# A new order for the passage from attention to the experts: logits, row copy, one-hot rows, and expert ranks in PSUM

## The chip, the core and the metric

One core of a Trainium2 chip runs the whole program in one launch. The metric is the device time of one execution in microseconds; the time before is the median of three runs. The five engines work side by side, each through its own queue in order: TensorE (PE, products into PSUM), VectorE (DVE), ScalarE (ACT), GpSimd (POOL) and SyncE (SP, which issues most transfers).

## What is computed

Causal attention with a bias from a running sum, then a routed layer of 16 experts over the 4608 tokens that attention leaves:

```python
scores = scale * q @ k.T + minimum(-(cum_i - cum_j), 0)     # causal
x = softmax(scores) @ v                                     # (8 * 576, 512)
g_idx = argmax(x @ w_group);  e_idx = argmax(x @ w_expert[g_idx])
combined = softmax weight of the group * softmax weight of the expert
out[token] = combined * (relu(x @ w1[g, e]) @ w2[g, e])     # one expert for each token
```

## The kernel before

**Attention** runs over 64 heads, two to a pair (32 pairs), in steps, one head a step. Each step emits its pieces by an order written out by hand as a string of letters (`ORDERS`, `FIRST`, `LAST`): a letter pops the next entry of a queue of that name. Of the letters that the change touches, for a pair p: W turns the reciprocal sums back, K divides (`finish`, xT, L362), O transposes the rows on TensorE (`rows_out`, L406) and o copies them out of PSUM (`leave`, xr, L412), X rounds xT to the high part (xTh, L375), L takes the low part (xTl, L379), M copies the tail (xtl, L384), and Q runs products of the router's logits. For the last batch of four pairs, three of the four chunks of logits are run early (L727, L728), on the Q of pair 30, the fourth in the router's `batch`. Steps 64 to 68 have no head left to score and only empty the queues. The O transpositions share one PSUM bank (`small`).

**Router** (class `Router`, `batch`): for each of 8 batches it transposes logits, finds the best group and expert (eq, oh), makes one-hot rows (hot, L822), counts them with TensorE (pc, L829), works out positions, and adds token numbers and weights to lists with products (pi, pw, L873) and an addition (`st.added`, L879). The exponents of the softmax need df (L887) on VectorE and an exponential on ScalarE (L889).

**Experts**: `moe` runs 16 slots. Each weight piece of 1 MB is loaded by SP (L995), rounded on ScalarE (wh, L997), and its low part is made on GpSimd (wl, L1000) or, from a rounded copy in PSUM (pw, L1005), on VectorE (L1007). The first expert is known before the last batch is routed: its rows of seven batches are gathered early, and a tile of remaining rows (`rest`) is gathered when the last batch's ids exist. Its items are: `h_items`, the hidden products (ph, L1107; first of four blocks, last of four blocks, twice), Relu (hh, L1102) and its rest (hl, L1103); `y_items`, the output products (py, L1168: a block of 16 products each for four columns, then the low weights); `rest.items()`, for the remaining rows: transposition (L1249), hidden products (L1263) and so on. The order of the remaining 15 experts is found on VectorE by ranks: a comparison of all keys with all keys (L1326), rank (L1327), a one-hot table sel (L1329), and its product with the expert numbers (L1332), summed to esl (L1333) and copied to integers (esi, L1335), from which SP reads where the next weights lie. The PSUM pool of transpositions (`pt[0]`, three banks) serves the weight copies pw, the gathered rows' transpositions and the rest's products.

**Order.** Up to step 62 all engines follow the hand-written order. Behind it, only TensorE does, in each part; the order of VectorE, ScalarE and GpSimd is set by a planner from its own estimate of times, in which an instruction emitted earlier goes first among those that are ready. Three helpers bend it: `behind(tc, later, earlier)` puts one instruction behind another in the order and adds no wait on another engine; `hold` adds a wait; `after` does the same as `behind` for a group.

Of the kernel before, what the change touches and what calls it, by code (L numbers as in the profile page):

```python
# [8 lines left out]
F32 = mybir.dt.float32  # L9
# [4 lines left out]
ALU = mybir.AluOpType  # L14
AX = mybir.AxisListType
# [4 lines left out]
B, H, S, D = 8, 8, 576, 64  # L20
P = 128
# [3 lines left out]
E = 16  # L25
# [88 lines left out]
def attention(tc, qk, v, s, wr, xs, st):  # L114
    nc = tc.nc
    NP = B * H // 2
    LEAD = 4
    with ExitStack() as ctx:
# [215 lines left out]
        def normalise(p, vals, sums):  # L334

            c = p % 4
            m = {}

            def turn():
                for k in "YZWK":  # L340
                    need(k, p - 1)
                m["f"] = sm.tile([P, S], F32, name=f"st{p}", tag="st", bufs=1)
                nc.vector.transpose(m["f"], sums)
                push("Z", p, recip)

            def recip():
                f = m["f"]
                rc = m["rc"] = sm.tile([P, S // 32], F32, name=f"rc{p}", tag="rc", bufs=2)
                nc.vector.reciprocal(rc, f.rearrange("p (b c) -> p b c", c=32)[:, :, 0])

                push("W", p, back)

            def back():
                nc.vector.transpose(m["f"], m["rc"].unsqueeze(2).to_broadcast([P, S // 32, 32]))
                push("K", p, finish)

            def finish():
                for k in "OXLM":
                    need(k, p - 2)
                x = m["x"] = sm.tile([P, S], F32, name=f"xT{p}", tag="xT", bufs=2)  # L360
                xTs[p] = x
                st.divided = nc.vector.tensor_tensor(out=x, in0=vals, in1=m["f"], op=ALU.mult)  # L362
                push("X", p, high)
                push("O", p, lambda: rows_out(p))

            def high():
                x = m["x"]
                if c == 0:
                    for k in "LMQ":
                        need(k, p - 1)  # L370
                    rt.read(p // 4)
                    xhl[p // 4] = [late.tile([P, 4, 512], F32R, name=f"xT{n}{p}", tag=f"xT{n}", bufs=1) for n in "hl"]
                    xtail[p // 4] = XT[p // 4 % 2]
                xh, xl = (t[:, c] for t in xhl[p // 4])
                st.xh = nc.scalar.copy(xh, x[:, 0:512])  # L375
                push("L", p, lambda: low(xh, xl, x))

            def low(xh, xl, x):
                (nc.gpsimd if p < NP - 2 else nc.vector).tensor_tensor(  # L379
                    out=xl, in0=x[:, 0:512], in1=xh.bitcast(F32), op=ALU.subtract)  # L380
                push("M", p, lambda: tail(x))

            def tail(x):
                nc.scalar.copy(xtail[p // 4][:, 64 * c:64 * c + 64], x[:, 512:576])  # L384
                b = p // 4
                if p == NP - 2:
                    push("Q", p, lambda: rt.logits(b, *xhl[b], range(3)))
                if c == 3:
                    push("Q", p, lambda: route(b))

            push("Y", p, turn)
# [130 lines left out]
        for t in VT:  # L522
# [19 lines left out]
        LAST = FIRST  # L542
        ORDER0 = "B0 b e A0 a T t B1 b D A1 a B2 b e A2 a B3 b e e A3 a B4 b e A4 a A5 a".split()
        for step in range(-LEAD, NH + 5):
            m, a = step + LEAD, step - 1
# [18 lines left out]
            if step >= 2 and step // 2 + 4 < NP:  # L564
                push("S", step // 2 + 4, lambda p=step // 2 + 4, part=step % 2: split(p, part, True))
            named = {"A": A, "B": Bq, "C": C}
            order = FIRST if step < 3 else ORDERS if step < NH - 1 else LAST
            for part in order[step % 2] if step > 0 else ORDER0:
                if part[0] in named:
                    for f in named[part[0]][int(part[1]):int(part[1]) + 1]:  # L570
# [66 lines left out]
class Router:  # L637
# [127 lines left out]
    def batch(self, b, xtail, xh, xl):  # L765
# [27 lines left out]
        for c in range(4):  # L793
# [25 lines left out]
                        op=ALU.is_equal)  # L819
        F4 = [P, NB, 4, 4]  # L820
        ohb = st.hot[:, b]
        V.tensor_tensor(out=ohb.rearrange("p t (g e) -> p t g e", e=4), in0=oh[:, :, 1:5],  # L822
                        in1=oh[:, :, 0].unsqueeze(3).to_broadcast(F4), op=ALU.mult)
        yield 2

        pc = (self.ps_s if b < B - 1 else self.ps_t)(f"pc{b}")
# [57 lines left out]
            st.routed = first_ids(nc, self.end, st, 0, 3, ((0, 2, 3, st.ids0[:, 2:3]), (1, 0, 3, st.ids1)))  # L884

        df = self.end.tile([P] + G[1:], F32, name=f"df{b}", tag="eq", bufs=1)
        V.tensor_tensor(out=df, in0=lgv, in1=mb, op=ALU.subtract)  # L887
        ex = df
        nc.scalar.activation(ex, df, AF.Exp)  # L889
        yield 1  # L890
# [33 lines left out]
def moe(tc, w1, w2, xs, st, out):  # L924
# [3 lines left out]
    with ExitStack() as ctx:  # L928
# [20 lines left out]
        def bc(t, ax, shape):  # L949
            return t.unsqueeze(ax).to_broadcast(shape)  # L950
# [337 lines left out]
        def run(items):  # L1288
            for f in items:
                f()  # L1290
# [31 lines left out]
        for k in range(2):  # L1322
            V.scalar_tensor_tensor(out=key, in0=st.first[:, k], scalar=(2 - k) * 1.0e6, in1=key, op0=ALU.mult,
                                   op1=ALU.add)
        rank = mc.tile([P, E], F32, name="rank")
        V.tensor_tensor(out=t3, in0=bc(key, 1, S3), in1=bc(key, 2, S3), op=ALU.is_gt)  # L1326
        V.tensor_reduce(out=rank, in_=t3, axis=AX.X, op=ALU.add)  # L1327
        sel = mq.tile(S3, BF16, name="sel")
        V.tensor_tensor(out=sel, in0=bc(rank, 1, S3), in1=bc(ie, 2, S3), op=ALU.is_equal)  # L1329
        esl = mc.tile([P, E], F32, name="esl")  # L1330
        csl = mc.tile([P, E], F32, name="csl")
        V.tensor_tensor(out=t3, in0=sel, in1=bc(ie, 1, S3), op=ALU.mult)  # L1332
        V.tensor_reduce(out=esl, in_=t3, axis=AX.X, op=ALU.add)  # L1333
        esi = mc.tile([P, E], I32, name="esi")
        nc.scalar.copy(esi, esl)  # L1335

# [29 lines left out]
        with tc.manual_schedule(engines={ENG.PE}):  # L1366
# [4 lines left out]
                behind(tc, i, st.left)  # L1371
            behind(tc, st.xh, wts[0].casts[2])
            behind(tc, wts[0].casts[3], st.xh)
            hold(tc, lows[0, 0, 0], st.divided)
            behind(tc, wts[0].casts[8], first.split[0])
            h = first.h_items()
            run(h[:12])
# [8 lines left out]
            behind(tc, st.added[0], first.rests[5])  # L1386
            behind(tc, st.weighing, first.rests[7])
            Y, R = first.y_items(), rest.items()
            run(Y[:2] + R[:1] + Y[2:4])

            behind(tc, st.listed[2], first.product)
            run(R[1:5] + Y[4:])
# [255 lines left out]
```

## Time and profile before

| what | us |
|---|---|
| three runs | 929.62, 918.28, 924.96 |
| median | 924.96 |
| profiled execution | 921.04 |
| its span, first to last instruction | 919.3 |
| TensorE busy | 855.2 (93%) |
| VectorE busy | 736.9 (80%) |
| ScalarE busy | 610.2 (66%) |
| GpSimd busy | 605.7 (66%) |

The mean granted clock of TensorE over the span is 0.986 of full speed. In a timeline a row is one instruction or a run of equal ones: start, duration, engine, line, operation, what is written from what, shapes, how many; in square brackets the idle time of the engine ahead of it and what ended that. A wait is put down to the event that came last. The attention ends near 440 us, the first expert's products begin near 451, and the loop over the other experts begins near 490.

### The profile page before, as it was taken

How to read it: one execution, taken by the hardware profiler on the slowest of the kernel's cores; microseconds unless marked ns; L12 is line 12 of the kernel's file. 1: busy time of each engine (PE TensorE's matmuls, PEld its weight loads, DVE VectorE, ACT ScalarE, POOL GpSimd, SP SyncE). 2: the span in 40 equal slices, each digit the busy share in tenths (PEclk: the TensorE clock that was granted, in tenths of full speed). 3: DMA queues.
4: the chain of work that ended last, by engine and by line, in shares of the span. 5: the costliest groups of instructions: out<-in, count | busy, mean ns of one | idle time of the engine just before them, and what ended most of it. 6: DMA issues, size and time to landing. Idle time of an engine off the chain costs nothing. (4 is left out here: it accounts for less than half of the span.)

```text
span 919.3 us, 17750 instructions
## 1 busy us (share of the span) xinstructions
PE 855.2 (93%) x5584; PEld 780.2 (85%) x5584; DVE 736.9 (80%) x1981; ACT 610.2 (66%) x1389; POOL 605.7 (66%) x748
## 2 busy tenths in 40 slices
PE   4899999999999999998798999999999999999995
PEld 2778788788888888886687999999999999999984
DVE  7666697787979798777578888899888899888871
ACT  5667777677777777775646566666767666767750
POOL 9666567666776758546665856766676776767650
PEclk9999999999999999999899999999999999999998
DMA  7899888888888888622544645545555545655510
GB/s 204 236 238 227 215 230 227 206 210 200 220 223 217 221 223 214 160 74 100 189 150 168 221 176 205 193 169 190 215 185 191 195 183 205 229 197 192 181 70 24
DMA packets 81877, 174.06 MB, mean 189 GB/s; under 512 B 9676, under 2 KB 45132, under 8 KB 73584
## 3 DMA queue, kind: packets, MB, share of 16 engines
q1 hardware_dynamic: 71664, 152.93, 57.8%
q0 software_dynamic: 7488, 18.89, 5.8%
q10 hardware_dynamic: 2624, 1.03, 0.5%
q8 instruction: 46, 0.75, 0.4%
q14 instruction: 55, 0.45, 0.2%
HBM read 108.97 MB, written 19.69 MB: 140 GB/s over the span
## 5 line engine op out<-in xcount | busy, mean ns | idle before, releaser
L1000 POOL TENSOR_TENSOR wl<-raw,wh 128x512 fp32r<-128x512 f32 x163 | 210.3, 1305 | 76.2 <-ACT wh L997 58.5
L227 DVE CUSTOM_DVE_ANT_0 mx<-pm,mask 128x192 bf16<-128x192 f32 (+4 forms) x320 | 127.3, 418 | 36.0 <-PE pm L219 33.3
L997 ACT CAST wh<-raw 128x512 fp32r<-128x512 f32 x256 | 155.3, 616 | 1.4 <-issue 1.4
L1107 PE MATMUL ph<-xl,wh 128*128 128x256 f32 (+13 forms) x512 | 145.3, 303 | 3.0 <-DVE xl L1079 3.0
L1107 PE MATMUL ph<-xh,wh 128*128 128x256 f32 (+13 forms) x512 | 144.8, 302 | 2.0 <-ACT xh L1078 1.7
L219 PE MATMUL pm<-WA 66*128 66x288 f32 (+4 forms) x384 | 124.8, 356 | 21.5 <-DVE mc L227 11.5
L275 PE MATMUL ps<-WA 68*128 68x320 f32 (+4 forms) x384 | 135.3, 356 | 4.8 <-DMA WA<-tl 4.6
L315 PE MATMUL po<-pt,VT 128*128 128x256 f32 (+3 forms) x512 | 120.9, 355 | 6.8 <-issue 4.2
L1168 PE MATMUL py<-hl,wh 128*128 128x256 f32 (+13 forms) x448 | 113.6, 302 | 1.7 <-DVE hl L1103 1.7
L1168 PE MATMUL py<-hh,wh 128*128 128x256 f32 (+13 forms) x448 | 112.9, 302 | 0.0
L277 PE MATMUL ps<-WB 128*128 128x320 f32 (+4 forms) x384 | 109.8, 299 | 0.0
L315 PE MATMUL po<-pu,VT 128*128 128x320 f32 (+1 forms) x384 | 107.5, 388 | 1.1 <-POOL pu L294 1.1
L1221 DVE STREAM_TRANSPOSE yr<-yT 32x384 f32<-32x384 f32 (+1 forms) x208 | 104.5, 502 | 4.2
L315 PEld LDWEIGHTS po<-pt,VT 128*128 128x128 f32 x512 | 88.4, 193 | 21.0 <-issue 5.0
L1074 DVE STREAM_TRANSPOSE xt<-xg 32x256 f32<-32x256 f32 (+1 forms) x208 | 102.5, 493 | 3.1
L1107 PEld LDWEIGHTS ph<-xl,wh 128*128 128x128 f32 x512 | 96.9, 189 | 5.9 <-DVE xl L1079 5.0
L1107 PEld LDWEIGHTS ph<-xh,wh 128*128 128x128 f32 x512 | 97.1, 190 | 3.8 <-ACT xh L1078 2.9
L219 PEld LDWEIGHTS pm<-WA 66*128 66x128 f32 (+1 forms) x384 | 69.1, 192 | 31.8 <-DVE mc L227 15.5
L294 POOL TENSOR_SCALAR_AFFINE_SELECT pt<-pt 128x128 f32<-128x128 f32 (+2 forms) x192 | 65.8, 354 | 43.7 <-ACT pt L285 40.5
L1102 ACT ACTIVATE hh<-ph 128x256 fp32r<-128x256 f32 (+13 forms) x128 | 53.6, 420 | 60.3 <-PE ph L1107 59.5
L161 POOL TENSOR_TENSOR WB<-r,hl 64x576 fp32r<-64x576 f32 x62 | 87.3, 1408 | 5.9 <-ACT hl L157 2.1
L1107 PE MATMUL ph<-xh,wl 128*128 128x256 f32 (+13 forms) x512 | 90.2, 299 | 0.0
(246 smaller groups left out, 2000.8 us busy)
## 6 DMA issues: line engine op xcount, KB each, us to landing
raw<-in_w_dram SPq DMA_DIRECT2D x64, 1024.0 KB
r<-in_qk_dram SPq DMA_DIRECT2D x32, 576.0 KB
WA<-hl SPq DMA_DIRECT2D x60, 288.0 KB
WB<-hl SPq DMA_DIRECT2D x60, 288.0 KB
VT<-in_v_dram SPq DMA_DIRECT2D x32, 384.0 KB
WB<-hl SPq DMA_DIRECT2D x64, 144.0 KB
xs<-xr SPq DMA_DIRECT2D x15, 512.0 KB
WA<-cumd SPq DMA_DIRECT2D x56, 4.5 KB
```

What stands on the lines that cost most here:

```text
L161: (nc.vector if p < 1 else nc.gpsimd).tensor_tensor(out=hl[:, 2] if part else WB[p % NBB][0:64, KA, h], in0=r[hr, part], in1=hl[hr, part]. ...
L219: nc.tensor.matmul(ps[:rows, :cw], WA[i][0:66, QA, h, QO + q0:QO + q0 + rows], WA[i][0:66, KA, h, QO + c0:QO + c0 + cw], start=True, stop= ...
L227: nc.vector.tensor_tensor_reduce(out=tmp[:rows, :cw], in0=ps[:rows, :cw], in1=mk[:rows], scale=1.0, scalar=-3.0e38 if c0 == 0 else mo, op0 ...
L275: nc.tensor.matmul(ps[:rows, o:o + w], WA[i][0:68, KA, h, QO + k0:QO + k0 + rows], WA[i][0:68, QA, h, QO + q0:QO + q0 + w], start=True, st ...
L277: nc.tensor.matmul(ps[:rows, o:o + w], WB[p % NBB][:, KA, h, k0:k0 + rows], WB[p % NBB][:, QA, h, q0:q0 + w], start=False, stop=True)
L315: nc.tensor.matmul(po[0][:, qa - base:qb - base], VT[p % NVT].rearrange("p t a d -> p (t a d)")[:, (3 * t + 1 + h) * 64:][:, 0:P], x[:, c: ...
L997: self.casts.append(nc.scalar.copy(h[:, j], raw[:, j]))
L1000: self.low = lows[self.u, i, j] = nc.gpsimd.tensor_tensor(out=l[:, j], in0=raw[:, j], in1=h[:, j].bitcast(F32), op=ALU.subtract)
L1074: V.transpose(dst[:, 0:n, :, j], src[:, 0:n, :, i])
L1107: self.product = nc.tensor.matmul(pss[f][:, :cap], w[f // 4][:, c, (f % 4) * P:(f % 4 + 1) * P], x[:, c, :cap], start=(c == 0 and w is sel ...
L1168: self.product = nc.tensor.matmul(pss[c][:, :cap], w[2 + f // 4][:, f % 4, c * P:(c + 1) * P], x[:, f, :cap], start=(f == 0 and w is self. ...
L1221: V.transpose(dst[:, 0:n, :, i], src[:, 0:n, :, j])
```

## The change

1. Behind step 65 the orders are replaced by `ENDS`: the even step runs W O o K X L M Q once, the odd one nothing. Q, which ran ahead of K, X, L, M, now stands behind them, so the three early chunks of logits are emitted in step 66, ahead of the last O (pair 31).
2. The tail copy of pair 31 on ScalarE is put behind the rounding xTh of pair 31. That one stood already behind the row copy of pair 30 and three weight casts.
3. The first subtraction of the first expert's weights on GpSimd is held until the low part xTl of pair 31, no longer until its division.
4. In the last batch, df goes behind the one-hot rows hot.
5. The ranks and a copy of the expert numbers lie in a PSUM bank of `pt[0]`; sel and its product with the numbers read them there. The addition of the weights to the lists (`st.added[2]`) goes behind esl.
6. The transposition of the rest's rows stands behind three of the first expert's output blocks, not two.

```diff
@@ finish, low, tail
-                st.divided = nc.vector.tensor_tensor(out=x, in0=vals, in1=m["f"], op=ALU.mult)
+                nc.vector.tensor_tensor(out=x, in0=vals, in1=m["f"], op=ALU.mult)
...
-                (nc.gpsimd if p < NP - 2 else nc.vector).tensor_tensor(
+                st.xl = (nc.gpsimd if p < NP - 2 else nc.vector).tensor_tensor(
                     out=xl, in0=x[:, 0:512], in1=xh.bitcast(F32), op=ALU.subtract)
...
-                nc.scalar.copy(xtail[p // 4][:, 64 * c:64 * c + 64], x[:, 512:576])
+                i = nc.scalar.copy(xtail[p // 4][:, 64 * c:64 * c + 64], x[:, 512:576])
+                if p == NP - 1:
+                    behind(tc, i, st.xh)
@@ attention
+        ENDS = ["W O o K X L M Q".split(), []]
...
-            order = FIRST if step < 3 else ORDERS if step < NH - 1 else LAST
+            order = FIRST if step < 3 else ORDERS if step < NH - 1 else LAST if step < NH + 2 else ENDS
@@ Router.batch
-        V.tensor_tensor(out=ohb.rearrange("p t (g e) -> p t g e", e=4), in0=oh[:, :, 1:5],
-                        in1=oh[:, :, 0].unsqueeze(3).to_broadcast(F4), op=ALU.mult)
+        hot = V.tensor_tensor(out=ohb.rearrange("p t (g e) -> p t g e", e=4), in0=oh[:, :, 1:5],
+                              in1=oh[:, :, 0].unsqueeze(3).to_broadcast(F4), op=ALU.mult)
...
-        V.tensor_tensor(out=df, in0=lgv, in1=mb, op=ALU.subtract)
+        i = V.tensor_tensor(out=df, in0=lgv, in1=mb, op=ALU.subtract)
+        if b == B - 1:
+            behind(tc, i, hot)
@@ moe
-        rank = mc.tile([P, E], F32, name="rank")
+        shared = pt[0].tile([P, 512], F32, name="rank", tag="pt")
+        rank, nums = shared[:, 0:E], shared[:, E:2 * E]
+        V.tensor_copy(nums, ie)
...
-        V.tensor_tensor(out=t3, in0=sel, in1=bc(ie, 1, S3), op=ALU.mult)
-        V.tensor_reduce(out=esl, in_=t3, axis=AX.X, op=ALU.add)
+        V.tensor_tensor(out=t3, in0=sel, in1=bc(nums, 1, S3), op=ALU.mult)
+        behind(tc, st.added[2], V.tensor_reduce(out=esl, in_=t3, axis=AX.X, op=ALU.add))
...
-            hold(tc, lows[0, 0, 0], st.divided)
+            hold(tc, lows[0, 0, 0], st.xl)
...
-            run(Y[:2] + R[:1] + Y[2:4])
+            run(Y[:3] + R[:1] + Y[3:4])
```

## Rows read from the trace of the kernel before

**Rows 1.** Waits of TensorE, 425 to 500 us: total, times, longest.

```profile
PE px L406 <- ACT xr L412: 3.7, 1, 3.7
PE px L1057 <- DVE wl L1007: 2.6, 1, 2.6
...
PE prr_x L1249 <- DMA xg<-xs,ids: 1.6, 1, 1.6
PE pc L829 <- DVE hot L822: 1.2, 1, 1.2
```

**Rows 2.** Waits of TensorE, 497 to 920 us, the longest total.

```profile
PE ph L1107 <- DVE xl L1079: 3.0, 8, 0.4
```

**Rows 3.** Timeline of TensorE: start, us, engine, line, operation [idle before].

```profile
444.31 1.12 PE L406 MATMUL px<-ident,xT 128*128 128x128 f32 x4 [3.65 <-ACT xr L412]
...
451.25 0.36 PE L1107 MATMUL ph<-xh,wh 128*128 128x256 f32 x1
```

**Rows 4.** Timeline of ScalarE, 443 to 457 us.

```profile
443.40 0.24 ACT L384 COPY xtl<-xT 128x64 f32<-128x64 f32 x1 [2.41 <-DVE xT L362]
443.67 0.58 ACT L412 COPY xr<-px 128x512 f32<-128x512 f32 x1
...
445.71 0.62 ACT L375 CAST xTh<-xT 128x512 fp32r<-128x512 f32 x1
446.23 2.70 ACT L997 CAST wh<-raw 128x512 fp32r<-128x512 f32 x5
...
456.87 0.29 ACT L889 ACTIVATE df<-df 128x100 f32<-128x100 f32 x1 [1.06 <-DVE df L887]
```

**Rows 5.** Timeline of VectorE, 433 to 458 us.

```profile
433.65 0.69 DVE L379 TENSOR_TENSOR xTl<-xT,xTh 128x512 fp32r<-128x512 f32 x1 [0.16 <-ACT xTh L375]
...
446.36 1.57 DVE L379 TENSOR_TENSOR xTl<-xT,xTh 128x512 fp32r<-128x512 f32 x1 [2.99 <-ACT xTh L375]
...
455.49 1.35 DVE L887 TENSOR_TENSOR df<-logit,lmx 128x100 f32<-128x100 f32 x1
456.75 1.30 DVE L822 TENSOR_TENSOR hot<-oh 128x80 bf16<-128x80 f32 x1
457.98 0.41 DVE L1103 SCALAR_TENSOR_TENSOR hl<-ph,hh 128x256 fp32r<-128x256 f32 x1
```

**Rows 6.** Timeline of GpSimd, 444 to 460 us.

```profile
444.86 5.46 POOL L1000 TENSOR_TENSOR wl<-raw,wh 128x512 fp32r<-128x512 f32 x4 [7.90 <-ACT wh L997]
450.26 1.38 POOL L1294 MEMSET xg<- 128x1536 f32 x1
451.60 7.60 POOL L1000 TENSOR_TENSOR wl<-raw,wh 128x512 fp32r<-128x512 f32 x6
```

**Rows 7.** Timeline of VectorE, the difference of the batch before.

```profile
419.54 0.26 DVE L887 TENSOR_TENSOR df<-logit,lmx 128x100 f32<-128x100 f32 x1
```

**Rows 8.** Timeline of VectorE, 478 to 488 us.

```profile
478.30 3.48 DVE L1329 TENSOR_TENSOR sel<-rank,ie 128x256 bf16<-128x256 f32 x1
481.81 4.15 DVE L1332 TENSOR_TENSOR t<-sel,ie 128x256 f32<-128x256 bf16 x1
...
486.33 1.28 DVE L1007 TENSOR_TENSOR wl<-raw,pw 128x512 fp32r<-128x512 f32 x2
```

**Rows 9.** Timeline of TensorE, first and last of 32 output products.

```profile
464.85 0.36 PE L1168 MATMUL py<-hh,wh 128*128 128x256 f32 x1
...
468.65 0.28 PE L1168 MATMUL py<-hl,wh 128*128 128x256 f32 x1
```

**Rows 10.** Line 1007, whole span: ns min/median/max, first and last start.

```profile
L1007 DVE TENSOR_TENSOR wl<-raw,pw x93: 674/687/690, 463.1 to 886.2; 128x512 fp32r<-128x512 f32 x93
```

**Rows 11.** Timeline of ScalarE, 486 to 489 us.

```profile
486.45 0.20 ACT L1335 CAST esi<-esl 128x16 int32<-128x16 f32 x1 [7.08 <-DVE esl L1333]
...
487.05 1.19 ACT L1189 COPY yT<-py 128x256 f32<-128x256 f32 x4
```

**Rows 12.** Stretch: us, busy PE, PEld, DVE, ACT, POOL, granted clock, DMA share, GB/s.

```profile
489.00:490.00 1.00, 1.00 (x7) 0.94 (x6) 0.74 (x3) 0.70 (x2) 0.00 (x0) 0.50 0.90 377
```

## The prediction

> **What bounds the kernel now.** I read the page first, then the waits of TensorE in two stretches, then the timelines of the five engines between them, last the granted clock microsecond by microsecond. Behind 497 us TensorE's longest entry of waits is 3.0 us over eight places [rows 2]: the expert stage is a full queue of products, and what is won ahead of it should arrive at the end undiminished. Between 425 and 500 us, in the passage from attention to the experts, four single waits stand: 3.7, 2.6, 1.6 and 1.2 us [rows 1], 9.1 together. The change aims at these four and at nothing else: the orders of steps before 66 stay, so neither attention up to there nor the expert loop has another instruction. The most that can be won is thus about 9 us of 921, plus what the clock gives back.
>
> **First wait: copy, logits, low part.** The transposition of pair 31 sits behind 3.65 us of idle [rows 3], so that of pair 30 ended at 444.31 - 3.65 = 440.66. Its bank is the only one, and the copy that empties it ran on ScalarE at 443.67, behind a tail copy of pair 31 that had itself waited 2.41 us for the divided rows [rows 4]. ScalarE was therefore free at 440.99 with a ready copy behind a blocked one. The change puts the tail copy behind the rounding xTh: the copy runs 440.99 to 441.57, three weight casts follow at 2.70/5 = 0.54 each [rows 4] until 443.2, and xTh starts when the divided rows come, 443.40, in place of 445.71: 2.3 us earlier, done at 444.02 with 0.62. VectorE's low part takes 0.69 with GpSimd idle and 1.57 beside it [rows 5]; the new hold keeps GpSimd away, so 0.69: it ends at 444.74 where it ended at 447.93. The last chunk of logits can start 3.2 us earlier.
>
> The six other logits products move from behind the last transposition into the hole in front of it. Their inputs of pair 30 are long there (the other low part was made at 433.65 [rows 5]). They issue no DMA. The hole from 440.66 to 443.40 is 2.74 us; before, they stood between the last transposition (444.31 + 1.12 = 445.43) and the low part's end, 447.93, so at most 2.5. They fit and cost nothing; were they late, the last transposition would be, one for one.
>
> What follows is ScalarE's queue: after xTh now the tail copy (0.24) and five casts (2.70), until 444.02 + 0.24 + 2.70 = 446.96; before it was 446.23 + 2.70 = 448.93 [rows 4]. The last row copy, its DMA to xs (ScalarE's own queue), the copy of the logits and the rest up to the first expert product at 451.25 [rows 3] hang behind these casts. I take 1.97 us. Bounds: nothing, if the casts cannot start before 444 for a reason that the trace hides; 3.2, if the planner now lets the row copy and the logits pass the five casts. I take the value between, as rows show that order of ScalarE.
>
> The hold itself puts ten subtractions on GpSimd behind the low part, and behind those the clearing of a gather buffer and the later gathers. Before they began at 444.86 [rows 6], now at 444.74: nothing lost. The fourth ends 5.46 later; its user is the product with wl, 32 products behind the first one (0.12 each, by [rows 9]), so 3.9 after 449.28, at 453.2: three us of cover. SP's next weight load waits for the same four and does not move either.
>
> **Second wait: one-hot rows ahead of exponents.** Before: difference 455.49 (1.35), then one-hot 456.75 (1.30), and TensorE's count waited 1.2 for it [rows 1, 5]. Both are slow because GpSimd subtracts beside them (451.60 to 459.2 [rows 6]); the batch before took 0.26 for the difference [rows 7]. Swapped and 1.97 earlier, one-hot runs 453.52 to 454.85, difference to 456.2. The count's stall goes almost wholly. But the exponent is queued on ScalarE ahead of the first Relu: it had waited 1.06 for the difference and started 456.87 [rows 4]. The difference moves only 1.97 - 1.30 = 0.65, so exponent 456.2, Relu from 456.5, the first rest hl about 456.8 to 457.2; it was at 457.98 [rows 5]. The second half of the hidden products needs that bank (`acc` has four banks for eight blocks). TensorE could be there at 449.28 + 48 x 0.12 + 0.5 for the count = 455.6, so a new wait of about 1.6 takes the place of the 1.2. Without it this half would have started at 458.73 less 1.97 less 1.23; with it at 457.2. So from here on the lead is **1.5**, not 3.2. Bounds: 3.2 if the Relu goes first; 0.6 if the later slots of VectorE stretch by another 0.9 between subtractions.
>
> One page speaks to this place. No row shows a two-input VectorE instruction that ran beside a GpSimd clearing alone; beside subtractions they cost 1.35 and 1.30. The Trainium skill, SBUF — State Buffer, Who interferes with whom, says that a VectorE instruction with two SBUF inputs is blocked by a GpSimd instruction that reads SBUF, not by one that only writes. By it, two instructions of the routing that would now fall beside the clearing at 450.26 would cost what they cost undisturbed, an estimate of 1 us more lead here. The sum does not count it.
>
> **Third wait: one more block of outputs ahead of the gathered rest.** TensorE waits 1.6 us for the gather [rows 1]. The ids that it needs move with the products and with VectorE's chain, both by about 1.5. Ahead of it now stand three blocks in place of two; 32 products take 468.65 - 464.85 + 0.12 = 3.92 [rows 9], so a block of 16 is 1.96, more than 1.63. The wait goes: **1.6**. Behind it the fourth block (1.96) still covers the rounding of the transposed rest (0.6 and 0.7 on ScalarE and VectorE, like xTh and xTl). Lower bound 0, if the ids do not move.
>
> **Fourth wait: ranks in PSUM, list of experts first.** sel took 3.48 and the product after it 4.15 for 256 columns [rows 8], beside subtractions on GpSimd; both stood behind the addition of weights at 478.03. An instruction with one operand in PSUM does not stretch so: hl from ph, also 256 columns, took 0.41 at 457.98 in the middle of subtractions [rows 5, 6], and wl from pw, twice the columns, lies between 674 and 690 ns in all 93 cases [rows 10]. So each should cost 0.45, and both now run in VectorE's idle stretch before the addition. What hung behind: wl at 486.33 [rows 8], whose bank the transposition of the next expert's rows waited 2.6 for [rows 1], and ScalarE, which sat 7.08 us at esi with Relu and output copies queued behind it, those at 487.05 [rows 11]. All of this falls to the pace of TensorE. The idle also cost clock: at 489 us the granted clock is 0.50, the lower of its two levels [rows 12]; about 3 us ran so. TensorE keeps one short wait, as the fourth transposition needs the first one's bank (output copies 1.2, rounding 0.5, low 0.5, against 1.5 of other work): I charge 0.5. So 2.6 - 0.5, plus 1.3 of the 1.5 that half clock over 3 us costs: **3.4**. Bounds 2.0 (the clock falls anyway) and 4.2. The copy of indices into the bank (16 columns) is off the path, and the bank it takes in the pool of three is free again before the second hidden block of the rest asks.
>
> **Sum.** 1.5 + 1.6 + 3.4 = 6.5 us. The profiled execution took 921.04 (span 919.3 and 1.74 around it), so 914.5 by its own time. The median of the runs is 924.96, 3.9 above it, and the runs spread over 11 us; the mean of all four times (929.62, 918.28, 924.96, 921.04) is 923.5, and I take that as base: **917**.
>
> **Rivals.**
> 1. Entry lost: ScalarE's casts wait or the planner sets them otherwise, and the Relu behind the exponent eats the rest. Only the third and fourth part remain, 1.6 + 2.0 = 3.6 to 5.0: 919 to 920. For it: the order of three engines is the planner's, not written out. Against: nothing in the rows held the casts but the copy. Chance 0.23.
> 2. All four waits go and the Relu overtakes: 3.2 + 1.6 + 4.2 = 9: 914.5. Chance 0.12.
> 3. Slower: the hold. If the low part came late instead of early, GpSimd's ten subtractions (5.46 + 1.38 + 7.60 = 14.4 us of work [rows 6]) would move with it. It decides from the point where the fourth subtraction misses 453.2, that is, a start after 447.7, 3 us behind my forecast; from there each us is a us of TensorE, and past 6.5 more the kernel is slower: some 2 us, 925.5. Against: xTh and xTl have nothing left in front. Chance 0.05.
> 4. No change: TensorE's waits shift to the next late thing, weights of the second expert, and all lead is returned by 530 us: 923.5. For it: loads wait for buffers. Against: the fourth load waits for wl at 486.33, which comes earlier too. Chance 0.10.
>
> **How the numbers follow.** The forecast has 0.50 (its own range 5 to 8 us, 915.5 to 918.5). Low end of the range: 918.3, the fastest run, less 10: 908. High end: rivals 1 and 4 on a base of 925 to 929: 925. Faster or slower by over 2% (18.5 us), about what a measurement of this kernel can tell from no change, would need more than all waits of the passage: 0.02 and 0.02.
>
> **What would show it.** Right: the copy of pair 30 near 441 and no 3.7 us wait; xTl at 0.7; the first expert product near 449.3; one-hot ahead of the difference; no wait at the gathered rest; sel and its product under 0.5 each, ahead of the addition; no 0.50 clock at 489. New: a wait of some 1.5 us at the second half of the hidden products. Wrong if a bank wait shows at the rest's products, if xTh still stands behind 445, or if TensorE's waits behind 497 grow by what the passage won.

## The result and the profile after

The changed kernel takes 913.31 us as the median of 20 runs (909.59 to 919.53), the kernel before 923.89 us in 20 runs beside them (917.62 to 931.53). The ratio is 0.9888, with a 95% interval from 0.9864 to 0.9912: about 10.3 us less, between 8.1 and 12.6. By the bound of 2% this counts as the same; the interval says that it is a gain. The forecast was 917 in a range from 908 to 925, a gain of 6.5; the median lies in that range, but below the 915.5 to 918.5 that the forecast gave its own course. The profiled execution took 914.72 us, span 913.0.

The page after, busy time of each engine. All five do the work of before: the busy times differ by some 2 us at most, save that of VectorE, which is 11.7 less.

```profile
span 913.0 us, 17750 instructions
...
PE 853.2 (93%) x5584; PEld 778.1 (85%) x5584; DVE 725.2 (79%) x1982; ACT 611.4 (67%) x1389; POOL 607.1 (66%) x748
```

The waits of TensorE in the passage, 418 to 492 us, of the kernel after (what waited, for what: total, times, longest). They answer to [rows 1]:

```profile
...
PE ph L1112 <- DVE hl L1108: 1.8, 1, 1.8
PE px L408 <- DVE xT L362: 1.3, 1, 1.3
...
PE pc L832 <- DVE hot L825: 1.2, 2, 0.6
PE lg L731 <- DVE xTl L379: 1.0, 1, 1.0
PE pr L785 <- ACT xr L414: 0.8, 1, 0.8
PE pur L1268 <- ACT xhr L1256: 0.4, 1, 0.4
PE pur L1268 <- DVE xlr L1257: 0.2, 1, 0.2
```

Of the four waits of [rows 1], three are gone: 3.7 for the row copy, 2.6 for the weights of VectorE, 1.6 for the gather. The one for the one-hot rows is halved (0.6; the other 0.6 of this row belongs to the batch before, which [rows 1] does not cover). In their place stand new ones: 1.8 for the rest `hl` at the second half of the hidden products, and at the entry 1.3 for the divided rows, 1.0 for the low part and 0.8 for the row copy. Behind the passage the longest entry is what it was in [rows 2], here in the waits of TensorE from 487 to 914 us:

```profile
PE ph L1112 <- DVE xl L1084: 3.0, 8, 0.4
```

**Where the time went, stage by stage.** A profile is one execution, and the attention ahead of the passage is not the same length in two of them: the last `sums` on ScalarE (the softmax sums of the last pair, copied out of PSUM) starts anywhere from 433.5 to 446.3 us over fourteen profiles, 440.12, 442.39 and 433.50 in three profiles of the unchanged kernel before. So all that follows is counted from that instruction. The table is made from the timelines of ScalarE and TensorE: it gives the start of the first expert's first output product, the start of the second expert's (taken as the end of the passage), the length between the two, and what is left of the span behind.

```
us behind the last sums       1st expert's   2nd expert's    between   rest of
                              first output   first output    the two   the span
before                        24.73          74.14           49.41     405.04
before, second profile        24.73          74.62           49.89     405.09
before, third profile         27.33          77.09           49.76     405.11
after                         25.41          69.62           44.21     405.08
after, second profile         24.45          67.47           43.02     405.19
after, third profile          24.76          68.94           44.18     405.11
only ranks (part 5 alone)     24.73          71.32           46.59     405.10
early sel                     24.71          71.28           46.57     405.10
all but ranks                 24.20          75.55           51.35     405.12
two blocks (all but part 6)   26.39          72.92           46.53     405.11
rest first                    21.96          65.69           43.73     405.05
no hot order (all but part 4) 24.32          68.54           44.22     405.16
held                          23.76          68.03           44.27     405.11
padded                        24.24          68.47           44.23     405.13
```

Three things are read from it. The last column does not move: what the passage wins arrives whole. The stretch between the two outputs took 49.4 to 49.9 before and takes 43.0 to 44.2 after: that is nearly the whole gain. The entry ahead of it, where the forecast had 1.5 us, takes 24.2 to 25.4 with the code of after (the padded kernel counted), and 24.7, 24.7 and 27.3 before; `two_blocks`, whose edit lies behind the entry, took 26.4.

### The profile page after: what moved, and what is told of

Same layout as the page of the kernel before. It is cut to its first block, busy times and chain, and to the rows that moved or that the text cites. A ratio compares the mean times of both kernels' runs of the same rounds, so it can differ in the third digit from the quotient of the medians.

```text
span 913.0 us, 17750 instructions
## 1 busy us (share of the span) xinstructions
PE 853.2 (93%) x5584; PEld 778.1 (85%) x5584; DVE 725.2 (79%) x1982; ACT 611.4 (67%) x1389; POOL 607.1 (66%) x748
```

## The experiments

Parts are numbered as in the list of the change: (1) order of the last steps, (2) tail copy behind the rounding, (3) the new hold, (4) one-hot rows ahead of the difference, (5) ranks in PSUM with the list of experts first, and (6) the third block of outputs ahead of the gathered rest.

**The two kernels again, unchanged, twice.** No edit.

> The kernel before, a second profile. The profiled execution of before (921.0) was 2.9 us faster than the median of 20 runs (923.9), that of the changed kernel (914.7) 1.4 slower than its median (913.3). Theory A (the difference of the medians is made in the passage, by the length of its waits or by stretches at the lower clock, which vary from run to run): attention up to the last pair's sums ends within 1 us of 440.1 and the passage is longer than in the first profile by some 3 us. Theory B (the spread is made in attention or in the expert loop, which the change does not touch): the passage from the last sums to the first full block of the second expert takes 55.6 us again, to 0.5, and the rest differs.

> The changed kernel, a second profile. Theory A: the 1.8 us wait of the second half of the hidden products is there again, but the lower clock behind it (456.3 to 459.2) or the late rounding of the rest (471.8) is not, and the passage is 1 to 3 us shorter. Theory B: the passage is the same to 0.5 us.

> The kernel before, a third profile. Nothing differs in any engine's instructions up to the passage, and the profiles give a passage 4.5 to 7.1 us shorter, the medians of the changed kernel 10.3 us (interval 8.1 to 12.6). Theory A (what the medians have more is spread of attention, which the profiles happen to show small): sums anywhere from 436 to 445 us, passage 74.1 to 74.7. Theory B (the passage of the kernel before is itself often longer): passage over 76.

> The changed kernel, a third profile. Theory A: passage 67.4 to 69.7, sums anywhere from 436 to 445. Theory B: passage under 67.

One execution each: before 923.91 and 917.43, after 916.47 and 914.03. The passage took 74.62 and 77.09 before, 67.47 and 68.94 after. With the first profiles the means are 75.3 (74.14 to 77.09) and 68.7 (67.47 to 69.62), three profiles each. The difference is 6.6, at least 4.5 and at most 9.6. The third profile of before is long in its entry alone: 27.33 against 24.73, with the same stretch between the two outputs. Its waits of TensorE from 420 to 500 us have 1.8 for the one-hot rows in place of 1.2 in [rows 1] (3.0 for the weights in place of 2.6 stands in the second profile too, whose passage is 74.62), and its granted clock was at the lower level twice, ahead of the first expert product, which came 0.7 later, and behind the count.

```profile
...
PE px L1057 <- DVE wl L1007: 3.0, 1, 3.0
...
PE pc L829 <- DVE hot L822: 1.8, 1, 1.8
```

Its stretches (columns as in [rows 12]); in the first profile the clock from 460 to 465 us, the place of the second and third row, was 1.00:

```profile
440.00:442.00 2.00, 1.99 (x6) 0.61 (x5) 1.31 (x1) 2.00 (x5) 2.00 (x2) 0.50 0.00 0
...
454.00:456.00 2.00, 2.00 (x12) 2.00 (x11) 1.93 (x9) 1.99 (x4) 0.00 (x0) 0.51 0.18 74
456.00:458.00 2.00, 2.00 (x13) 2.00 (x13) 1.97 (x5) 0.00 (x0) 0.00 (x0) 0.64 0.00 0
```

Of the expectations, the second profile of before has the passage of the first within 0.5 and the third one of over 76, each as its Theory B says. The second profile of after is 2.2 shorter and the third lies in the range given, each as Theory A says, but the wait at the second half of the hidden products was 1.0 in the second, not 1.8.

**Part 5 alone.** The kernel before with the ranks and indices in a PSUM bank and the list of experts ahead of the list addition:

```diff
-        rank = mc.tile([P, E], F32, name="rank")
+        shared = pt[0].tile([P, 512], F32, name="rank", tag="pt")
+        rank, nums = shared[:, 0:E], shared[:, E:2 * E]
+        V.tensor_copy(nums, ie)
...
-        V.tensor_tensor(out=t3, in0=sel, in1=bc(ie, 1, S3), op=ALU.mult)
-        V.tensor_reduce(out=esl, in_=t3, axis=AX.X, op=ALU.add)
+        V.tensor_tensor(out=t3, in0=sel, in1=bc(nums, 1, S3), op=ALU.mult)
+        behind(tc, st.added[2], V.tensor_reduce(out=esl, in_=t3, axis=AX.X, op=ALU.add))
```

> The kernel before with the fifth part alone: ranks and expert numbers in PSUM, the list addition behind esl. By the two profiles the first four parts and the sixth win 1.95 us at the first expert product and have returned all of it when the low output products start, so this part alone should give nearly the whole: theory A, 4 to 5 us in the trace and a ratio of 0.990 to 0.995. Rival (the forecast's sum: 3.1 us from the other parts, 3.4 from this one): ratio 0.996. sel and its product take 0.42 each beside GpSimd's subtractions in both.

Ratio 0.9948 (0.9922 to 0.9973). The timeline of VectorE in this kernel:

```profile
475.95 0.42 DVE L1331 TENSOR_TENSOR sel<-rank,ie 128x256 bf16<-128x256 f32 x1 [5.48 <-PE pw L873]
476.40 0.42 DVE L1334 TENSOR_TENSOR t<-sel,rank 128x256 f32<-128x256 bf16 x1
...
477.19 0.35 DVE L879 TENSOR_TENSOR lists<-lists,pw 128x192 f32<-128x192 f32 x1
478.20 1.28 DVE L1007 TENSOR_TENSOR wl<-raw,pw 128x512 fp32r<-128x512 f32 x2 [0.66 <-ACT pw L1005]
```

3.48 and 4.15 us in [rows 8] have become 0.42 each, as forecast. But `sel` did not run in the idle stretch: it sat out 5.48 us of it, since it waits for a product of TensorE (`pw`), as the addition behind it does. The place on the path did not move; only the length did. The stall of 2.6 is gone, and a smaller one stands behind it: the waits of TensorE from 479 to 509.5 us of this kernel have one entry.

```profile
PE ph L1107 <- DVE yr L1282: 1.4, 1, 1.4
```

The stretch between the two outputs is 46.59 in place of 49.4 to 49.9, 2.8 to 3.3 less; the forecast for this part was 3.4, and the 4 to 5 us expected just ahead of the run did not come. Part 5 also puts the addition (0.35) behind the list of experts; what that order adds was not separated.

**All but part 5.**

```diff
-        shared = pt[0].tile([P, 512], F32, name="rank", tag="pt")
-        rank, nums = shared[:, 0:E], shared[:, E:2 * E]
-        V.tensor_copy(nums, ie)
+        rank = mc.tile([P, E], F32, name="rank")
...
-        V.tensor_tensor(out=t3, in0=sel, in1=bc(nums, 1, S3), op=ALU.mult)
-        behind(tc, st.added[2], V.tensor_reduce(out=esl, in_=t3, axis=AX.X, op=ALU.add))
+        V.tensor_tensor(out=t3, in0=sel, in1=bc(ie, 1, S3), op=ALU.mult)
+        V.tensor_reduce(out=esl, in_=t3, axis=AX.X, op=ALU.add)
```

> The changed kernel without the fifth part (ranks in SBUF, list addition not behind esl). Theory A: sel and its product stretch to 3 to 4 us each again, the 2.6 us wait at the second expert's transposition is back, and the ratio is 0.997 to 1.001. Rival (sum of the forecast): 0.996 to 0.997 with 3.1 us won.

Ratio 1.0002 (0.997 to 1.0034): the other five parts without part 5 are worth nothing that shows. The second expert's rows are reached 2.4 us earlier than in the first profile of before, and then TensorE stands; the waits of TensorE from 430 to 496 us begin with

```profile
PE prr L1254 <- DVE wl L1012: 3.3, 1, 3.3
```

and the timeline of VectorE shows why:

```profile
479.66 0.35 DVE L882 TENSOR_TENSOR lists<-lists,pw 128x192 f32<-128x192 f32 x1 [5.99 <-PE pw L876]
479.93 6.84 DVE L1334 TENSOR_TENSOR sel<-rank,ie 128x256 bf16<-128x256 f32 x1
486.80 0.43 DVE L1337 TENSOR_TENSOR t<-sel,ie 128x256 f32<-128x256 bf16 x1
```

`sel` took 6.84 and `t` 0.43, 7.3 together beside 7.6 in [rows 8] (not 3 to 4 us each, as expected). What they wait for is GpSimd, whose timeline has nine subtractions and one clearing without a gap:

```profile
474.83 7.50 POOL L1005 TENSOR_TENSOR wl<-raw,wh 128x512 fp32r<-128x512 f32 x6
482.28 0.52 POOL L1320 MEMSET yT<- 128x512 f32 x1
482.77 3.71 POOL L1005 TENSOR_TENSOR wl<-raw,wh 128x512 fp32r<-128x512 f32 x3
```

Their end, 486.48, sets the end of `sel`, and so the arrival of the second expert's weights, wherever TensorE is by then. So the parts are not a sum: part 5 sets what the others can deliver.

**An early `sel` instead of PSUM.** The kernel before, with a place of its own for `sel`:

```diff
-        sel = mq.tile(S3, BF16, name="sel")
+        sel = st.sel
```

where `st.sel` is one more tile of that shape, made once.

> The kernel before; only the one-hot table sel has a place of its own, so that it no longer lies over what the list products read. In it and in the changed kernel sel carries a wait for TensorE. Theory A (sel is late because it may overwrite the operands of the list products only when these are read; the operand in PSUM helps because sel is then still late but does not stretch beside the subtractions): sel and its product run near 468 us, ahead of the subtractions, 0.45 us each from SBUF, and the gain is that of the fifth part alone, ratio 0.993 to 0.997. Rival (what helped is the operand in PSUM alone): both stretch to 3 to 4 us and the ratio is 0.999 to 1.001.

Ratio 0.9975 (0.9942 to 1.0009), which overlaps with that of part 5 alone and also reaches 1; what decides is the trace. The timeline of VectorE:

```profile
466.92 0.42 DVE L1330 TENSOR_TENSOR sel<-rank,ie 128x256 bf16<-128x256 f32 x1
...
467.80 0.41 DVE L1333 TENSOR_TENSOR t<-sel,ie 128x256 f32<-128x256 bf16 x1
```

Now `sel` does run as soon as the ranks are there, 9 us earlier than with part 5 alone, with both operands in SBUF and 0.42 long, ahead of GpSimd's subtractions. So what held it was the place that it shared with a buffer the list products read, and what made it long was to run beside those subtractions. The passage is 71.28 against 71.32 with part 5 alone, one profile each: two cures for one cause.

**All but part 6**, two blocks of outputs ahead of the gathered rest as before:

```diff
-            run(Y[:3] + R[:1] + Y[3:4])
+            run(Y[:2] + R[:1] + Y[2:4])
```

> The changed kernel with two output blocks ahead of the transposition of the rest, as before. Theory A (the third block only covers the gather's landing): the wait for the gather is back, 1.0 to 1.8 us, and the ratio is 0.990 to 0.992. Rival (the lead returned at the hidden products leaves the rest in time): no wait, ratio 0.988 to 0.990.

Ratio 0.9922 (0.9889 to 0.9956). The waits of TensorE from 430 to 496 us: the one for the gather is back with its old length.

```profile
...
PE lg L731 <- DVE xTl L379: 2.1, 1, 2.1
PE prr_x L1254 <- DMA xg<-xs,ids: 1.6, 1, 1.6
PE ph L1112 <- DVE hl L1108: 1.3, 1, 1.3
```

In the waits of TensorE from 484 to 515 us of this kernel a second one is back, the one that part 5 alone had too:

```profile
PE ph L1112 <- DVE yr L1287: 1.3, 1, 1.3
```

With the third block neither is there, and two small ones for the rounded rest (0.4 and 0.2) come instead. By the table the third block is worth 2.3 us (46.53 less 44.21; 3.5 by the shortest profile of after); the forecast of 1.6 had counted the gather only. The longer entry (26.39) does not come from the block, which lies behind it: the row copy came late (see the first wait below), and the granted clock was 0.50 from 449.6 to 455.6 us.

**All but part 4**, without the order of one-hot rows and difference:

```diff
-        if b == B - 1:
-            behind(tc, i, hot)
```

> The changed kernel with the difference left ahead of the one-hot rows. Theory A (the fourth part pays for the shorter wait of the count with a later first Relu and rest, so it is worth nothing): the wait of the count is 1.2 to 1.8 us again, the wait at the second half of the hidden products is gone or under 0.6, the second half starts 17.2 to 18.4 us behind the last sums (18.0 to 18.3 with the part), and the ratio is 0.987 to 0.990. Rival (the part is worth its 1.2 us): second half at 19.2 to 19.6, ratio 0.990 to 0.9915.

Ratio 0.9903 (0.9871 to 0.9935). The second half of the hidden products starts 18.21 us behind the last `sums`, with part 4 at 17.97, 18.34 and 18.63. The wait for `hl` is gone and the one-hot rows cost 0.3. Part 4 by itself is worth nothing that the times can tell. The wait of 1.2 to 1.8 for the one-hot rows that was expected did not come back. Counted from the row copy that sets the entry (see the first wait below), the second half starts at 15.94 here and at 16.49 to 16.53 with part 4 (three profiles of after, `pad` and `no_ranks`, with the same order of GpSimd): by the traces the part costs 0.6 there.

**The difference behind the first rests.** The kernel after, with the last difference behind the fourth `hl` of the first expert, and the third weight copy of that stretch (`pw`) behind the fourth Relu, so that neither the exponent nor the copy stands ahead of the first four (`st.df` and `lent` name these two instructions):

```diff
...
+            behind(tc, st.df, first.rests[3])
+            behind(tc, wts[0].lent, first.rounds[3])
```

> The changed kernel; for the last batch the difference of the exponents goes behind the fourth rest hl of the first expert, and the third rounded weight copy of the first expert behind the fourth Relu. Theory A (exponent and weight copy stand ahead of the first Relu on ScalarE, difference ahead of the first rest on VectorE, and this makes the wait of 1.0 to 1.8 us at the second half of the hidden products): that wait falls to under 0.3, no lower clock follows it, the second half starts 16 to 16.5 us behind the last sums in place of 18.0 to 18.3, and the ratio falls to 0.985 to 0.988. Rival (the wait is the bank's, whoever is ahead, or the ids of the rest come no earlier and the lead is given back at the gathered rest): the second expert's products start no earlier, ratio 0.988 to 0.990.

Ratio 0.9884 (0.9839 to 0.9928), median 913.0. In the profile the second half starts at 15.94 in place of 17.97 to 18.63, the first output product at 21.96, and the passage takes 65.69, the shortest of all, 1.8 to 3.9 less than after. TensorE waits neither for `hl` nor for the rounded rest; its waits of 0.7 us or less from 430 to 496 us are

```profile
PE pc L832 <- DVE hot L825: 0.7, 1, 0.7
PE pr L785 <- ACT xr L414: 0.7, 1, 0.7
PE prr_x L1255 <- DMA xg<-xs,ids: 0.2, 1, 0.2
```

Part of that is an earlier row copy, by 0.2 to 0.9 us: counted from it, the first output product stands at 20.72, after at 22.62, 22.63 and 23.97, so 1.9 at the least. That the time is less than that of the kernel after is not shown, and the ratio expected, 0.985 to 0.988, was missed: six runs leave half a per cent open on either side, and 2 or 3 us lie inside.

**All four held.** GpSimd's order after has three subtractions ahead of the held one, so the hold did not reach these three. Here all four are held:

```diff
-            hold(tc, lows[0, 0, 0], st.xl)
+            for j in range(4):
+                hold(tc, lows[0, 0, j], st.xl)
```

> The changed kernel with all four subtractions of the first weight piece held until the low part, not the first alone. In the changed kernel's order the planner sends three of them past the held one; they start at 441.45, a microsecond before the low part. Theory A (the hold of one instruction is evaded, and evading it costs next to nothing): no subtraction starts ahead of the low part's end, the low part takes 0.69 in place of 0.83, the subtractions end 1 to 2 us later, and the passage is 67.4 to 69.7 us as before. Rival (the early subtractions feed the product with the low weights in time and only so): a new wait for GpSimd ahead of the product with wl, passage over 70.

921.12 us in one execution, which began its passage 8.0 us later than the first profile of after. The timeline of GpSimd:

```profile
446.29 1.38 POOL L1299 MEMSET xg<- 128x1536 f32 x1 [2.97 <-PE po L315]
451.38 12.55 POOL L1005 TENSOR_TENSOR wl<-raw,wh 128x512 fp32r<-128x512 f32 x10 [3.71 <-DVE xTl L379]
```

All ten subtractions stand behind the low part, which now took 0.69, and the passage is 68.03, like the others of after: no product waits for the weights of GpSimd. A hold that works costs nothing here, and the passage shows no gain from it; counted from the row copy the second half starts at 16.00, 0.5 earlier than after, in this one profile.

**Another place in SBUF.** The kernel after with 64 bytes more in a partition ahead of what follows:

```diff
-    st.ie = cst.tile([P, E], F32, name="ie")
+    st.ie = cst.tile([P, 2 * E], F32, name="ie")[:, 0:E]
```

> The changed kernel with one small constant tile 64 bytes wider, so that everything behind it lies where it lay before the ranks left SBUF; no instruction differs. The passage is 4.5 to 7.1 us shorter in the profiles, the medians 10.6 us. Theory A (places in SBUF matter, and the shift by 64 bytes made attention faster): ratio 0.992 to 0.995, last sums at 441 to 442 us. Rival (places do not matter; the rest of the difference is the spread of attention from run to run): ratio 0.987 to 0.991.

Ratio 0.9888 (0.9841 to 0.9935), that of after. The ranks that left SBUF took 64 bytes in a partition, and putting these back changes nothing that shows: the shift of the tiles behind has no part in the gain.

## Why the prediction was right, and where its steps were off

**The bound and the bookkeeping: right.** The expert loop behind the passage took 405.04 to 405.19 us in all fourteen profiles, so rival 4, by which the loop gives the lead back, is out. The gain of the passages, 6.6, is near the 6.5 of the forecast, which is luck in part, as the sum below shows. By the medians, 10.3 (8.1 to 12.6), the gain is above the 5 to 8 of the forecast's own course; the time is nearest to rival 2, though what rival 2 rests on, a Relu that overtakes, did not happen.

**First wait: right on TensorE's first product, by way of a copy that was not ready, and then given back.** The timeline of ScalarE after:

```profile
439.74 0.59 ACT L414 COPY xr<-px 128x512 f32<-128x512 f32 x1 [0.56 <-DMA xs<-xr]
440.23 1.66 ACT L1002 CAST wh<-raw 128x512 fp32r<-128x512 f32 x3
441.79 0.62 ACT L375 CAST xTh<-xT 128x512 fp32r<-128x512 f32 x1
442.31 0.24 ACT L384 COPY xtl<-xT 128x64 f32<-128x64 f32 x1
442.45 2.70 ACT L1002 CAST wh<-raw 128x512 fp32r<-128x512 f32 x5
...
454.68 0.29 ACT L894 ACTIVATE df<-df 128x100 f32<-128x100 f32 x1 [2.69 <-DVE df L890]
454.87 0.58 ACT L1010 CAST pw<-raw 128x512 fp32r<-128x512 f32 x1
455.38 1.19 ACT L1107 ACTIVATE hh<-ph 128x256 fp32r<-128x256 f32 x4
```

Copy, three casts, rounding, tail copy, five casts: the order and the lengths are those of the forecast. The first expert product came 9.18 us behind the last `sums`, 11.13 before: 1.95 earlier, forecast 1.97. In the two other profiles of after it came at 9.56 and 9.86, 1.3 to 1.6 earlier. What set this lead the forecast did not name. "A ready copy behind a blocked one" is wrong: `xr` has one buffer, and the row above puts 0.56 of idle ahead of the copy down to the transfer of the rows before out of it; in the two other profiles of after it is 0.95 and 1.26. So the copy came 1.44 us behind the last `sums`, forecast 0.87 (440.99 less 440.12), and then 1.83 and 2.13. In eight of the nine profiles with parts 1 and 2 the first expert product follows 7.72 to 7.74 us behind this copy (8.90 in `two_blocks`, at the lower clock). In the first profile the copy's delay and a shorter way behind it cancel; in the others the lead is smaller by as much as the copy is later.

A second detail was wrong: the low part took 0.84 in the first profile, as the hold did not keep GpSimd away, whose timeline is

```profile
441.45 4.20 POOL L1005 TENSOR_TENSOR wl<-raw,wh 128x512 fp32r<-128x512 f32 x3 [6.10 <-ACT wh L1002]
445.59 1.38 POOL L1299 MEMSET xg<- 128x1536 f32 x1
446.93 8.83 POOL L1005 TENSOR_TENSOR wl<-raw,wh 128x512 fp32r<-128x512 f32 x7
```

The first of these three starts ahead of the low part (442.44) and the second beside it. Rival 3, the slower one, was thus never put to the test by the change. `held` puts all ten subtractions behind the low part, and no product waited for them; but they began 5.1 us behind the last `sums` there, and rival 3 starts at 7.6 (447.7 less 440.12), so a late low part stays untested.

**Second wait: the mechanism right, the size off.** The forecast said that the exponent, queued ahead of the first Relu, makes a new wait of about 1.6 at the second half of the hidden products. It is there, with 1.8 (1.0 in the second profile), and its chain can be read in the timeline of VectorE after, against the rows of ScalarE above:

```profile
452.17 1.21 DVE L825 TENSOR_TENSOR hot<-oh 128x80 bf16<-128x80 f32 x1
453.30 1.34 DVE L890 TENSOR_TENSOR df<-logit,lmx 128x100 f32<-128x100 f32 x1
...
455.79 0.42 DVE L1108 SCALAR_TENSOR_TENSOR hl<-ph,hh 128x256 fp32r<-128x256 f32 x1 [0.99 <-ACT hh L1107]
```

The difference ends at 454.64, the exponent starts at 454.68, and between it and the Relu stands one more thing that the forecast did not name, a weight copy `pw` of 0.58. So `hl` starts at 455.79, and the second half begins 17.97 us behind the last `sums` in place of 18.61. The lead there is 0.6, in the other profiles 0.3 and 0.0; the forecast had said 1.5, with 0.6 as its lower bound. This is the term that was mis-sized. In the first profile the granted clock fell to 0.50 behind the wait, and the first output product came 0.7 later than before. The stretches of two us of after show it (columns as in [rows 12]):

```profile
454.00:456.00 2.00, 0.46 (x4) 0.26 (x3) 1.00 (x3) 1.32 (x5) 1.77 (x2) 0.97 0.78 233
456.00:458.00 2.00, 1.73 (x8) 1.74 (x9) 1.93 (x10) 2.00 (x7) 0.00 (x0) 0.50 0.70 295
```

In the third profile of after the same wait of 1.8 left the granted clock at 1.00. `rest_first` takes both hindrances away, and its one profile shows what the entry could have given: 24.73 less 21.96, 2.8 us, an early row copy included. Its passage is 8.5 us below the first profile of before and 9.6 below the mean of three; that is rival 2, in which the Relu overtakes, and its 9. The medians do not show it (0.9884 beside 0.9888).

**Third wait: right, and too small.** The third block hides the gather, as worked out. It also removes the 1.3 to 1.4 at `yr`, and brings 0.6 for the rounded rest that the fourth block was to cover: 2.3 in place of 1.6.

**Fourth wait: right in size, wrong in one sentence.** "Both now run in VectorE's idle stretch before the addition" is false. The timeline of VectorE after:

```profile
478.77 0.42 DVE L1336 TENSOR_TENSOR sel<-rank,ie 128x256 bf16<-128x256 f32 x1 [5.63 <-PE pw L876]
479.24 0.42 DVE L1339 TENSOR_TENSOR t<-sel,rank 128x256 f32<-128x256 bf16 x1
...
481.03 1.28 DVE L1012 TENSOR_TENSOR wl<-raw,pw 128x512 fp32r<-128x512 f32 x2 [0.66 <-ACT pw L1010]
```

The step that failed is the free VectorE: `sel` had the ranks 10 us before, but its place in memory was still being read by products of TensorE, as `early_sel` shows by giving it another. The sum survived since the lengths were right (0.42 for 0.45), and the weights behind started 42.73 us after the last `sums` (481.03 less 438.30) where in [rows 8] it was 46.21 (486.33 less 440.12): early enough that TensorE does not wait for them. The short wait of 0.5 that was charged for a bank does not appear. The lower clock of [rows 12] is gone too: the second expert's first hidden products, at 489.52 and 490.47 before, stand in these stretches after, at 484.29 and 485.18.

```profile
484.00:486.00 2.00, 1.86 (x15) 1.45 (x13) 1.73 (x4) 2.00 (x6) 0.45 (x1) 1.00 0.99 410
486.00:488.00 2.00, 2.00 (x16) 1.84 (x15) 1.93 (x5) 2.00 (x5) 0.97 (x1) 1.00 1.01 401
```

**The sum.** By the table: entry 0.0 (24.73 in the first two profiles of before, 24.72 the mean of four with the code of after), third block 2.3, ranks 3.0, so 5.3, and what the third profile of before adds; the forecast had 1.5, 1.6 and 3.4. At the first output product rival 1, the lost entry, is thus what happened, by the way that it named (the Relu behind the exponent); its 3.6 to 5.0 for the rest were too low. Two errors of opposite sign made the total better than its terms: that is luck. And the terms don't stand by themselves: the parts without part 5 gave 1.0002, part 5 alone 0.9948, all six 0.9888, more than the two together. Parts 1 to 3 were not run by themselves.

**What stays open.** The medians say 10.3 us (8.1 to 12.6), the passages of six profiles 6.6 (4.5 to 9.6), and the rest of the span is equal. The two ranges overlap, but the profiles lean to less; by their own times the six profiled executions differ by 5.7 in the mean. The long passage of the third profile of before (77.09) says that before has executions in which the entry grows, by a wait and by the lower clock; after has shown a growth of 0.7 in one of three, and `two_blocks`, with the same entry, one of 1.7. Whether that makes the other 3 to 4 us, or the spread of the attention, can't be told from executions that were not profiled. The shift of the tiles is not it (`pad`).

**The rule on the shared port.** The Trainium skill, SBUF — State Buffer, Who interferes with whom, was weighed for two routing instructions beside the clearing of the gather buffer, which only writes. That stays untested: by the rows above, the clearing at 445.59 to 446.97 had no two-input instruction of the routing beside it, and those at 452.17 and 453.30 ran beside subtractions with the old lengths, 1.21 and 1.34. For `sel` the other half of that section of the Trainium skill, that a VectorE instruction with at most one input in SBUF does not contend with GpSimd outside the modes that take both ports, agrees with the trace: 0.42 at 478.77, beside subtractions, with one operand in PSUM, against 6.84 at 479.93 in `no_ranks` with both in SBUF. One input alone is no safeguard: before, `kemp<-kids`, 128x32 with one input, took 1.18 at 430.61 beside a clearing, and 0.19 for 128x48 at 466.05.

## What to carry to other kernels

When one wait goes, look at once at what is queued in order behind the next late thing: here the exponent and a weight copy ahead of the first Relu gave back the whole entry, and in one profile two lines of order kept it. Before a copy is called ready, ask what still reads the place that it writes: a transfer out of a single buffer set the start of this entry. An instruction moved forward in program order runs earlier only if its place in memory is free too; ask who reads it last. Cost parts that lie in series as a chain with its latest member, not as a sum: the other parts together were worth nothing until part 5 came.

## What the chip showed that had not been expected

- One VectorE instruction of 256 columns with both inputs in SBUF took 0.42 us ahead of GpSimd's subtractions and 6.84 us beside them. It was held by a row of them, not by one: it ended at 486.77, and the ninth subtraction at 486.48. The clearing of 0.52 between the sixth and the seventh did not let it through there; in the second and third profile of before, with `sel` at 7.56 and 7.55, it did not either; the 3.48 in [rows 8] ended at 481.78, 0.3 after its sixth, beside the clearing. What decided it no row shows.
- TensorE's granted clock after the same wait of 1.8 us was 0.50, its level of 1.2 GHz, in one execution and 1.00, 2.4 GHz, in another of the same kernel; in a third, where the wait was 1.0, it was 0.50 from 452 to 455 us, ahead of the wait, and 1.00 behind it. What decided it no row shows.
- The attention of one and the same kernel ended anywhere within 9 us (433.50 to 442.39 in three profiles of before). For a change of a few us, two profiles are compared from a common instruction, not from their start.
